# Storing the two parts of a split weight tile with one transfer instead of two, and the scheduler's length for that job halved

## The chip, the cores and the metric

One Trainium2 chip, one of its cores. The metric is the device time of one execution in microseconds (us), as the median of three runs. The engines of the core work side by side, each on its own list of instructions in a fixed order: TensorE (PE) multiplies matrices, VectorE (DVE), ScalarE (ACT) and GpSimd (POOL) do element-wise work, and SyncE (SP) issues nearly all DMA transfers, one after the other. An instruction that has to wait holds up everything behind it on its engine.

## The reference

Linear attention on 8 batches of 8 heads, 576 rows of 64, followed by two MLPs on the 4608 rows of 512 that the attention gives:

```python
q_s = exp(q - max(q, -1)); q_s /= sum(q_s, -1) + 1e-9
k_s = exp(k - max(k, 2));  k_s /= sum(k_s, 2) + 1e-9
kv  = einsum('bhsd,bhse->bhde', k_s, v)
x   = einsum('bhsd,bhde->bhse', q_s, kv)      # to rows of 8 * 64 = 512
h = x @ w_in;  x = (h * clip(h + 3, 0, 6) / 6) @ w_out
h = x @ w2_in; out = (h / (1 + exp(-h))) @ w2_out
```

The weights are float64 on the host (512x2048 and 2048x512 for each MLP), everything is computed at about float32 precision.

## The kernel before

Every operand of a large matrix product is split into a high part, rounded to TensorE's fast float32 form, and a low part, the rest; a product is three matmuls (high by high, high by low, low by high). The 4608 rows are nine blocks of 512 rows. The program has three stages, each written in a fixed order:

- `first_block`: attention of the first rows, conversion of the first MLP's weights, first MLP of block 0.
- `middle`: the first MLP for blocks 1 to 6, one step of 16 after the other (`mm1`, 12 matmuls of 512 columns, then the gate on ACT and DVE, then `mm2`, another 12). Beside it run the attention units of the later blocks (a unit is one block and one pair of heads) and the preparation of the weights for the last stage.
- `second_mlp`: the second MLP of all blocks, and the first one of blocks 7 and 8, by a Strassen-like scheme with seven products for eight. It reads its weights, in quarters and sums of quarters, from a buffer `ws` in HBM.

The weights for that last stage are made in `middle`. `Parts` converts two float64 row groups of the second MLP (`Conv`), `Resident` takes two of the first MLP's, and POOL forms four sums of quarters in place (`sums_in_place`). `Split` then makes the high part (`upper`, ACT), the low part (`lower`, DVE) and stores both (`store`, SP). One `Split` holds two quarters side by side, "halves" of 256 columns; each of them has a place of its own in `ws` (`slot`), and in each place the high part stands left of the low part. So a `store` is four transfers: two halves by two parts.

The order of `middle` comes from a list scheduler, `Plan`. Each job is added with an engine, a length in us, a key (its wanted place in time), the jobs it depends on, and the buffers it takes and gives back. `Plan.once` walks a clock forward and starts on every free engine the ready job of the lowest key whose buffers are free. Lengths in the table thus decide not only when an engine is free but when buffers come back, and so what is started next on every engine. `parted` adds the three jobs of a `Split`; the store's job gives back its `sp` buffers, and for some splits one of the five `t2k` buffers, small scratch tiles that nearly all other jobs share: the copies of a finished block (`finish_copy`, one for each of the four accumulators), the transposed queries (`q_blocks`), and the copies of attention results to be parked in HBM (`x_upper` for blocks from 4 on, tile `xq`).

Three lines of the attention units matter below. `x_mm` (L495) multiplies a unit's queries by its `kv` on PE into one of two PSUM tiles `pa`; `x_upper` (L505) copies that tile out on ACT into an `xq` tile, which frees it; `x_store` (L656) parks the copy. For later units the queries arrive by `q_load` (L479), four DMAs into a tile with the tag `qT`, of which there is one: the next unit's `q_load` has to wait until the `x_mm` that reads the tile is over.

Of the kernel before, what the change touches and what calls it, by code (L numbers as in the profile page):

```python
# [23 lines left out]
def f32(ap):  # L24
    return ap.bitcast(F32)
# [3 lines left out]
def efficient_attention_then_two_mlps(  # L29
# [11 lines left out]
    nc = tc.nc  # L41
# [41 lines left out]
    ws = dram.tile([2, 2, 4 * NF, P, DM], F32, name="ws")  # L83
# [87 lines left out]
    HALF = DM // 2  # L171

    def slot(o, i, part):
        if part == "A21":
            return 7 * NPR + i
        if o:
            return OUTER.index(part) * NPR + i
        if part == "A22":
            return 6 + 7 * i + 2 if i < NPR - 1 else 7 * NPR - 1
        return (0 if i == 0 else 6 + 7 * (i - 1)) + INNER.index(part) + (  # L180
            1 if i and part not in INNER[:2] else 0
        )
# [28 lines left out]
    class Split:  # L211
# [14 lines left out]
            nc.vector.tensor_tensor(out=self.lo, in0=self.src(), in1=f32(self.hi), op=ALU.subtract)  # L226

        def store(self):
            for h, name in enumerate(self.names):
                to = ws[self.ph, self.o, slot(self.o, self.i, name)]  # L230
                for a, t in enumerate((self.hi, self.lo)):
                    nc.sync.dma_start(  # L232
                        to[:, a * HALF : (a + 1) * HALF], f32(t)[:, h * HALF : (h + 1) * HALF]
                    )

    class Parts:

# [475 lines left out]
    class Plan:  # L713
# [7 lines left out]
        def add(self, eng, us, key, fn, deps=(), take=(), give=(), port=False):  # L721
            self.jobs.append(
                (eng, us, key, fn, [d for d in deps if d is not None], list(take), list(give), port)
            )
            return len(self.jobs) - 1
# [265 lines left out]
    def middle():  # L991
# [3 lines left out]
            a=2, h=2, g=1, r=1, z=1, qe=0, qT=1, ke=0, mx=2, m1=1, t2k=5, raw=0, sp=3, x=1, wi=0,  # L995
# [5 lines left out]
        def dma(us, key, fn, kb, deps=(), take=(), give=()):  # L1001
            return add("SP", us, key, (fn, kb * 1024), deps, take, give)
# [69 lines left out]
        def parted(split, key, deps, give=()):  # L1072
            sp = ["sp"] * (1 + split.keep)
            hi = add("ACT", 0.64, key, split.upper, deps, sp)
            lo = add("DVE", 0.72, key, split.lower, [hi], [], [], True)
            st = dma(1.4, key, split.store, 512, [lo], [], sp + list(give))
            return lo if split.keep else st

        for k in range(2 * NPR):
            o, i = divmod(k, NPR)  # L1080
            at = NF + 5.5 * k + 6 + WORK[k]
            p, done = Parts(i, o), []
            for n, c in enumerate(p.conv):
                ld = None
                if k:
                    ld = dma(
                        0.35, at - 2 + n, lambda i=i, n=n, o=o: load_w(1, 2 * i + n, o), 512, [], ["raw"]
                    )
                c0 = add("ACT", 0.67, at + n, c.scale, [ld], ["t2k"])
                c1 = add("DVE", 0.43, at + n, c.shift, [c0])  # L1090
                c2 = add("ACT", 0.67, at + n, c.scale_low, [c0], ["t2k"])
                c2 = add("DVE", 0.72, at + n, c.round, [c1, c2], [], ["t2k"], True)
                c3 = add("DVE", 0.72, at + n, c.sign, [c2], [], ["raw"], True)
                done.append(parted(p.split[n], at + n + 0.2, [c3]))
            for m, fn in enumerate(p.total):
                done = [add("POOL", 0.68, at + 1.3, fn, done, [], [], True)]
            for n in range(2):
                parted(p.split[2 + n], at + 1.4 + n, done, ["t2k"])
# [12 lines left out]
            for n in range(2):  # L1111
                done.append(parted(w.split[n], at + 2.5, done, ["raw"] if n else []))
# [602 lines left out]
```

## Time and profile before

| | us |
|---|---|
| median of three runs | 1578.06 (1576.75 to 1578.68) |
| profiled execution | 1579.01 |
| its span, first to last instruction | 1577.0 |
| PE busy | 1558.9 (99%) |
| DVE, ACT, POOL busy | 1111.1, 761.6, 487.8 |

The profiled execution is an execution of its own, 0.95 us above the median. The span is what the core's instructions cover; 2.0 us lie around it. TensorE ran at its full clock of 2.4 GHz throughout: the granted clock is 1.00. The trace has the start and length of each instruction, so a wait of PE can be read as the gap ahead of a matmul.

### The profile page before, as it was taken

Reading aid. Unit: us, or ns where it says so; the run is one execution under the profiler, and the core shown is the slowest. Engines: PE = TensorE matmul, PEld = TensorE weight load, DVE = VectorE, ACT = ScalarE, POOL = GpSimd, SP = SyncE. Lnnn points to the kernel's source line nnn. Section 1 sums busy time; section 2 is a strip of 40 time slices with the busy share of each in tenths; the row PEclk is TensorE's granted clock in tenths of the full one; section 3 lists DMA queues with packets and bytes.
Section 4 is the critical chain, followed back from the end, with each engine's and each line's share of the span. In section 5 each row is a group of like instructions: output and inputs, shape, how many; then the busy total and the mean of one; then the engine's idle time right before and its main releaser. Section 6 shows DMA issues by size and latency. Waiting matters only on the chain.

```text
span 1577.0 us, 22414 instructions
## 1 busy us (share of the span) xinstructions
PE 1558.9 (99%) x7352; PEld 1268.4 (80%) x7352; DVE 1111.1 (70%) x1792; ACT 761.6 (48%) x1360; POOL 487.8 (31%) x442
## 2 busy tenths in 40 slices
PE   7999999999999999999999999999999999999998
PEld 4777878887878888888888888888888888888887
DVE  7988577776767776554689569846986697677632
ACT  6886245454555554443365236533643464345322
POOL 4334224433424335321232243323223422440000
PEclk9999999999999999999999999999999999999999
DMA  9915977777778875755666786766668875879850
GB/s 267 345 44 185 313 216 227 238 215 215 223 215 246 235 227 166 238 174 193 192 222 218 214 226 224 249 217 192 237 203 218 220 252 192 227 226 370 260 127 27
DMA packets 391203, 342.82 MB, mean 217 GB/s; under 512 B 184880, under 2 KB 297520, under 8 KB 391088
## 3 DMA queue, kind: packets, MB, share of 16 engines
q1 hardware_dynamic: 389040, 340.32, 70.3%
q8 instruction: 58, 0.95, 0.2%
q10 hardware_dynamic: 2048, 1.08, 0.2%
q14 instruction: 57, 0.47, 0.1%
HBM read 247.20 MB, written 94.11 MB: 216 GB/s over the span
## 4 chain that ended last, share of the span: by engine, by line
PE 92%; DMA 2%; issue 1%; DVE 1%; POOL 1%; ACT 1%; SPq 1%; ACTq 0%; POOLq 0%; DVEq 0%
PE pb L1340 24%; PE pb L1499 24%; PE h L541 20%; PE y L613 17%; PE y L615 3%; PE pa L495 2%; PE pa L397 2%; DMA qraw<-in_q_dram 1%; DMA xr<-xq 0%; DMA xq<-xq 0%; POOL wi L164 0%; SPq L232 0%; PE pa L368 0%; PE pa L356 0%; ACT r L554 0%
## 5 line engine op out<-in xcount | busy, mean ns | idle before, releaser
L541 PE MATMUL h<-x,wi 128*128 128x512 f32 x1536 | 382.5, 396 | 1.6 <-POOL wi L164 0.9
L1340 PE MATMUL pb<-xo,ring 128*128 128x512 f32 x1680 | 383.0, 389 | 0.0
L1499 PE MATMUL pb<-gsp,ring 128*128 128x512 f32 x1680 | 382.4, 389 | 0.0
L1340 PEld LDWEIGHTS pb<-xo,ring 128*128 128x128 f32 x1680 | 315.4, 188 | 65.8 <-issue 0.5
L1499 PEld LDWEIGHTS pb<-gsp,ring 128*128 128x128 f32 x1680 | 315.4, 188 | 65.4
L541 PEld LDWEIGHTS h<-x,wi 128*128 128x128 f32 x1536 | 283.5, 188 | 65.9 <-POOL wi L164 2.0
L613 PE MATMUL y<-g,wo 128*128 128x512 f32 x1344 | 323.9, 390 | 0.6 <-ACT g L569 0.6
L613 PEld LDWEIGHTS y<-g,wo 128*128 128x128 f32 x1344 | 251.4, 188 | 53.6 <-ACT g L569 1.1
L1327 DVE TENSOR_TENSOR gsp<-g,gsp 128x512 fp32r<-128x512 f32 x240 | 183.0, 782 | 26.0 <-ACT gsp L1445 25.2
L1445 ACT CAST gsp<-g 128x512 fp32r<-128x512 f32 x240 | 143.6, 621 | 106.2 <-PE pb L1499 88.3
L578 DVE SCALAR_TENSOR_TENSOR h<-r,h 128x512 f32<-128x512 f32 x112 | 77.4, 691 | 80.3 <-ACT r L554 80.1
L554 ACT ACTIVATE r<-h 128x512 f32<-128x512 f32 x112 | 67.0, 598 | 133.4 <-PE h L541 131.7
L1327 POOL TENSOR_TENSOR xst<-xst 128x512 f32<-128x512 f32 x32 | 72.1, 2254 | 167.4 <-DVE xo L1327 85.3
L1327 DVE TENSOR_TENSOR g<-r,pb 128x512 f32<-128x512 f32 x96 | 65.7, 684 | 54.6 <-ACT r L1354 54.1
L1354 ACT ACTIVATE r<-pb 128x512 f32<-128x512 f32 x96 | 57.1, 595 | 97.0 <-DVE pb L1327 72.8
L1327 POOL TENSOR_TENSOR g<-g 128x512 f32<-128x512 f32 x40 | 53.6, 1340 | 148.6 <-DVE g L1327 123.4
L1327 POOL TENSOR_TENSOR s<-U,s 128x512 f32<-128x512 f32 x32 | 42.6, 1331 | 173.1 <-DVE U L1327 173.1
L569 ACT CAST g<-h 128x512 fp32r<-128x512 f32 x112 | 65.6, 586 | 59.8 <-DVE h L578 51.5
L572 DVE TENSOR_TENSOR g<-h,g 128x512 fp32r<-128x512 f32 x97 | 66.7, 688 | 28.8 <-ACT g L569 27.3
L1327 DVE TENSOR_TENSOR U<-pb,s 128x512 f32<-128x512 f32 x80 | 55.0, 688 | 17.0 <-PE pb L1340 14.9
L194 POOL TENSOR_TENSOR fa<-fa 128x256 f32<-128x256 f32 x64 | 49.9, 780 | 43.7 <-DVE sp L226 28.5
L427 POOL TENSOR_TENSOR qe<-qraw,qm 128x512 f32<-128x512 f32 x34 | 37.9, 1114 | 79.4 <-DVE qz L469 46.0
(158 smaller groups left out, 1721.2 us busy)
## 6 DMA issues: line engine op xcount, KB each, us to landing
ring<-ws SPq DMA_DIRECT2D x280, 512.0 KB, 3.9
ws<-sp SPq DMA_DIRECT2D x256, 128.0 KB, 2.6
wi_early<-in_moe_w_in_dram SPq DMA_DIRECT2D x16, 512.0 KB, 8.6
wo_early<-in_moe_w_out_dram SPq DMA_DIRECT2D x16, 512.0 KB, 9.6
wi_raw<-in_moe_w_in_dram SPq DMA_DIRECT2D x16, 512.0 KB, 5.0
ws<-w_sum SPq DMA_DIRECT2D x64, 128.0 KB, 2.2
ws<-fa SPq DMA_DIRECT2D x64, 128.0 KB, 2.3
wo_raw<-in_moe_w_out_dram SPq DMA_DIRECT2D x16, 512.0 KB, 4.4
```

The lines of the kernel that those rows point to most:

```text
L194: lambda to=to, x=x, y=y, op=op: nc.gpsimd.tensor_tensor(out=at[to], in0=at[x], in1=at[y], op=op)
L541: nc.tensor.matmul(h, w[:, a, c, :], x[:, e, c, :], start=(c == 0 and n == 0), stop=(c == NC - 1 and n == 2),)
L554: nc.scalar.activation(self.r, self.h, AF.Relu, bias=3.0)
L569: nc.scalar.copy(self.g[:, 0], self.r)
L572: nc.vector.tensor_tensor(out=self.g[:, 1], in0=self.r, in1=f32(self.g[:, 0]), op=ALU.subtract)
L578: nc.vector.scalar_tensor_tensor(out=self.h, in0=self.r, scalar=6.0, in1=self.h, op0=ALU.min, op1=ALU.mult)
L613: nc.tensor.matmul(y[c], w[:, a, cs], g[:, e, :], start=st, stop=sp)
L1327: (eng or nc.vector).tensor_tensor(out=out, in0=a, in1=b, op=how)
L1340: nc.tensor.matmul(to, ws_[:, a], e[:, c], start=p in ("P1", "P6", "P5") and c == 0 and m == 0, stop=c == 1 and m == 2, skip_group_check=True,
L1354: nc.scalar.activation(r, d[b, n, key], AF.Sigmoid)
L1445: nc.scalar.copy(t[0], source(p, i))
L1499: nc.tensor.matmul(d[b, p][m], w[:, a, m * P : (m + 1) * P], t[e], start=new and i == 0 and k == 0, stop=i == NPR - 1 and k == 2, skip_gro ...
```

## The change

`Split.store` issues two transfers in place of four. Each carries one part of both halves: 128 partitions by 2 places by 256 columns. The destination is a slice of `ws` with a step from the one place to the other. Where the second name's place lies ahead of the first, the halves are read in reverse order. The bytes and the places are the same as before. In the scheduler's table the store's length goes from 1.4 to 0.7 us.

```diff
         def store(self):
-            for h, name in enumerate(self.names):
-                to = ws[self.ph, self.o, slot(self.o, self.i, name)]
-                for a, t in enumerate((self.hi, self.lo)):
-                    nc.sync.dma_start(
-                        to[:, a * HALF : (a + 1) * HALF], f32(t)[:, h * HALF : (h + 1) * HALF]
-                    )
+            s0, s1 = (slot(self.o, self.i, name) for name in self.names)
+            to = ws[self.ph, self.o, min(s0, s1) : max(s0, s1) + 1 : abs(s1 - s0)]
+            to = to.rearrange("s p d -> p s d")
+            for a, t in enumerate((self.hi, self.lo)):
+                halves = f32(t).rearrange("p (h d) -> p h d", h=2)
+                nc.sync.dma_start(
+                    to[:, :, a * HALF : (a + 1) * HALF], halves if s0 < s1 else halves[:, ::-1]
+                )
...
-            st = dma(1.4, key, split.store, 512, [lo], [], sp + list(give))
+            st = dma(0.7, key, split.store, 512, [lo], [], sp + list(give))
```

With the new length the scheduler puts `middle` into another order on all engines. The new code is two lines longer, so line numbers from `store` on are two higher in the rows of the changed kernel (L495 becomes L497, L541 L543, L613 L615).

PE, the end of the first MLP's block 5 and the start of block 6, before. `y_5800` to `y_5803` are the accumulators of block 5, `y_6705` and on those of block 6; `pa<-qt` is an `x_mm`, and the number behind `kv` tells the units apart (97, 96 and 93 are three that follow each other):

```order
L613 MATMUL y_5803<-g,wo 128x512
L541 MATMUL h<-x,wi 128x512 x12
L613 MATMUL y_6705<-g,wo 128x512
...
L495 MATMUL pa<-qt,kv_97 128x512
L541 MATMUL h<-x,wi 128x512 x12
...
L495 MATMUL pa<-qt,kv_96 128x512
L541 MATMUL h<-x,wi 128x512 x12
...
L495 MATMUL pa<-qt,kv_93 128x512
L541 MATMUL h<-x,wi 128x512 x12
```

The same place of the changed kernel; `y_5695` is block 5's last accumulator there, `y_6679` block 6's first:

```order
L615 MATMUL y_5695<-g,wo 128x512
L543 MATMUL h<-x,wi 128x512 x24
L497 MATMUL pa<-qt,kv_97 128x512
L543 MATMUL h<-x,wi 128x512 x12
L497 MATMUL pa<-qt,kv_96 128x512
L497 MATMUL pa<-qt,kv_93 128x512
L615 MATMUL y_6679<-g,wo 128x512
```

Before, the three `x_mm` stood 66 and 40 rows apart inside block 6, with many `mm1` and `mm2` between them. Now they stand between the last `mm2` of block 5 and the first of block 6, one group of 12 matmuls between the first and the second and none between the second and the third.

SP at that place, in the changed kernel (`qt<-zd` is a `q_load`, the first one here for the second of these `x_mm`, the second one for the third; `yd<-o` stores a copy of `finish_copy`, `xq<-xq` is an `x_store`):

```order
L481 DMA qt<-zd 32x16x32 x4
L637 DMA yd<-o 128x512
L234 DMA ws<-sp 128x2x256
L234 DMA ws<-w_sum 128x2x256
L1205 DMA xo<-yd 128x2x512 x2
L234 DMA ws<-sp 128x2x256 x2
L481 DMA qt<-zd 32x16x32 x4
L637 DMA yd<-o 128x512
```

Before, the four `yd<-o` of block 5 stood in one group, and the `q_load`s beside them belonged to units whose `x_mm` came later. Now a `q_load` stands ahead of two of the `yd<-o`. The ACT copy (L507) that frees the `pa` tile of kv_97 waits for the landing of the last `yd<-o` shown, whose `t2k` buffer it writes into.

PE at the end of block 3, before (`k_turn` is L356, `k_spread` L368; between them DVE takes a maximum):

```order
L356 MATMUL pa<-ident,peaks 128x128
L495 MATMUL pa<-qt,kv_97 128x4x80
L495 MATMUL pa<-qt,kv_96 128x4x48
L541 MATMUL h<-x,wi 128x512 x3
L368 MATMUL pa<-ident,small 128x128
L541 MATMUL h<-x,wi 128x512 x9
```

and now:

```order
L543 MATMUL h<-x,wi 128x512 x12
L358 MATMUL pa<-ident,peaks 128x128
L370 MATMUL pa<-ident,small 128x128
L497 MATMUL pa<-qt,kv_97 128x4x80
L497 MATMUL pa<-qt,kv_96 128x4x48
L615 MATMUL y_4735<-g,wo 128x512
```

The `k_spread` follows its `k_turn` directly, and the `x_mm` follows the `k_spread`.

## Rows read from the trace of the kernel before

**Rows 1.** The page: the span, and busy time of each engine.

```profile
span 1577.0 us, 22414 instructions
PE 1558.9 (99%) x7352; PEld 1268.4 (80%) x7352; DVE 1111.1 (70%) x1792; ACT 761.6 (48%) x1360; POOL 487.8 (31%) x442
```

**Rows 2.** Busy time in stretches: us, each engine's busy time, PEclk, DMA share, GB/s.

```profile
130.00:600.00 470.00, 465.95 (x2415) 375.85 (x2412) 335.33 (x608) 233.33 (x427) 179.99 (x208) 1.00 0.78 233
600.00:722.00 122.00, 122.00 (x562) 98.75 (x561) 69.52 (x99) 55.24 (x94) 42.05 (x40) 1.00 0.57 178
750.00:1400.00 650.00, 650.00 (x2869) 538.41 (x2868) 484.46 (x705) 295.53 (x522) 208.97 (x135) 1.00 0.72 219
```

**Rows 3.** Who waited for whom, PE, 130 to 722 us: total, times, longest.

```profile
PE pa L356 <- DVE peaks L351: 2.6, 2, 2.1
PE y L613 <- ACT g L569: 0.6, 1, 0.6
PE pa L397 <- ACT ke L387: 0.4, 1, 0.4
PE pa L368 <- DVE small L362: 0.4, 1, 0.4
```

**Rows 4.** The page's DMA issues: count, KB each, median us to landing.

```profile
ws<-sp SPq DMA_DIRECT2D x256, 128.0 KB, 2.6
ws<-w_sum SPq DMA_DIRECT2D x64, 128.0 KB, 2.2
ws<-fa SPq DMA_DIRECT2D x64, 128.0 KB, 2.3
```

**Rows 5.** Timeline of SP, 150 to 200 us: start, length, instructions.

```profile
171.19 5.29 SPq L206 DMA_DIRECT2D ws<-wo  x8
176.59 2.08 SPq L232 DMA_DIRECT2D ws<-sp  x4
```

**Rows 6.** Landing of the stores of line L232 (the three groups of rows 4).

```profile
DMA to landing us min/median/max: 1.7/2.4/6.5
```

**Rows 7.** Landing of the stores of line L206 (256 KB each).

```profile
DMA to landing us min/median/max: 2.4/2.6/4.2
```

**Rows 8.** Timeline of PE, 595 to 722 us: start, length, instructions.

```profile
638.52 2.88 PE L613 MATMUL y<-g,wo 128*128 128x512 f32 x12
641.24 2.88 PE L541 MATMUL h<-x,wi 128*128 128x512 f32 x12
...
652.13 1.02 PE L495 MATMUL pa<-qt,kv 128*128 128x512 f32 x2
652.59 3.32 PE L541 MATMUL h<-x,wi 128*128 128x512 f32 x12
655.74 2.88 PE L613 MATMUL y<-g,wo 128*128 128x512 f32 x12
...
697.45 1.02 PE L495 MATMUL pa<-qt,kv 128*128 128x512 f32 x2
```

**Rows 9.** Timeline of SP, 600 to 722 us: the load behind the last x_mm.

```profile
698.50 2.83 SPq L479 DMA_DIRECT2D qt<-zd  x4
```

**Rows 10.** Line L479: duration ns min/median/max, first and last start us; landing.

```profile
L479 SPq DMA_DIRECT2D qt<-zd x108: 557/634/1432, 188.4 to 700.7; - x108
...
DMA to landing us min/median/max: 2.2/2.7/6.0
```

**Rows 11.** Landing of the stores of line L635 (yd<-o).

```profile
DMA to landing us min/median/max: 2.1/3.1/7.7
```

**Rows 12.** Timeline of ACT, 610 to 660 us: the idle time ahead in brackets.

```profile
653.24 0.59 ACT L505 COPY xq<-pa 128x512 f32<-128x512 f32 x1 [1.42 <-PE pa L495]
```

**Rows 13.** Timeline of PE, 425 to 470 us.

```profile
435.94 0.33 PE L356 MATMUL pa<-ident,peaks 128*128 128x128 f32 x1 [0.53 <-DVE peaks L351]
...
464.19 0.30 PE L356 MATMUL pa<-ident,peaks 128*128 128x128 f32 x1 [2.07 <-DVE peaks L351]
```

**Rows 14.** Timeline of PE, 130 to 137 us.

```profile
134.76 0.27 PE L356 MATMUL pa<-ident,peaks 128*128 128x128 f32 x1
135.42 0.32 PE L368 MATMUL pa<-ident,small 128*128 128x128 f32 x1 [0.38 <-DVE small L362]
```

**Rows 15.** Timeline of DVE, 130 to 137 us.

```profile
135.78 0.82 DVE L377 TENSOR_TENSOR ke<-kbuf,pa 128x640 f32<-128x640 f32 x1 [0.31 <-PE pa L368]
```

**Rows 16.** The page's groups: busy us, mean ns of one, idle before.

```profile
L578 DVE SCALAR_TENSOR_TENSOR h<-r,h 128x512 f32<-128x512 f32 x112 | 77.4, 691 | 80.3 <-ACT r L554 80.1
```

## The prediction

> **What bounds the kernel.** I read the page's busy times first: PE is busy 1558.9 us of 1577.0 [rows 1], so the other engines and the DMA queues count only where they make PE wait. The busy times by stretch tell where that can be: from 750 to 1400 us PE has no idle time at all, and from 600 to 722 none either [rows 2]. The order of the last stage and the order of the first do not change. What is left is `middle`, roughly 130 to 722 us, and there the view of who waited for whom shows all that PE loses to waits: 2.6 + 0.6 + 0.4 + 0.4 = 4.0 us, and none of it directly for a DMA [rows 3]. So nothing that the change makes cheaper can give back more than 4.0 us. What it can cost has no such limit, because PE works through its list in order and a wait that the new order creates stays in the time: the last stage has no idle time to absorb it.
>
> **The stores themselves.** The three groups of stores are 384 transfers of 128 KB [rows 4]; they become 192 of 256 KB. SP needs 2.08 us for the four of one split, and 5.29 / 8 = 0.66 us for one 256 KB store of another kind [rows 5]. Two of the new form are not in the trace; taking that row they cost 1.3 us, and the saving is 0.75 us for each of 96 splits, some 72 us of SP's time over 590. From the other side, if a new store cost as much as two old ones, nothing is saved. Either way PE gains 0 from it directly: none of its waits is for SP or for a store, and the 4.0 us above are the most that can come back. Landing hardly moves: 2.4 us at the median for a 128 KB store, 2.6 for a 256 KB store [rows 6, 7].
>
> The page "DMA: Bandwidth & Descriptors" of the Trainium skill, section "Rules for kernel authors", says to merge many small transfers into one large one, and its section "Anatomy of one DMA" gives each transfer a fixed cost of about 2.0 us. An estimate from that page of the Trainium skill would be one fixed cost less for each pair of stores. The trace bears out that the landing has a large fixed part, since twice the bytes land only 0.2 us later [rows 6, 7], but here the two old stores of a pair overlap, issued about 0.5 us apart [rows 5]: as their landings overlap, that fixed part is not saved per pair, and what the Trainium skill's page promises would show as a gain only where somebody waits for the landing. That is the first rival below.
>
> **The order, end of block 5.** Here the change costs. The three `x_mm` of kv_97, kv_96 and kv_93 now stand close together, and the queries of each arrive through the single `qT` tile. The price of one turn of that tile is in the trace. An `x_mm` started at 697.45 [rows 8]; SP began the next unit's four loads at 698.50 [rows 9], 1.05 us later, when PE had read the tile. The four took 2.83 us to issue, the last of them starting at 700.7; a load lands 2.2 us after its start at the least and 2.7 at the median [rows 10]. So the next `x_mm` cannot start before 700.7 + 2.7 - 697.45 = 5.95 us after the one before it (5.45 with the fastest landing). On PE an `x_mm` fills 0.89 us: from 652.13 to 655.74 it and 12 matmuls take 3.61, and 12 matmuls alone take 641.24 - 638.52 = 2.72 [rows 8].
>
> - Second `x_mm` (kv_96): between it and the first stand 12 matmuls. PE waits 5.95 - 0.89 - 2.72 = 2.34 us (1.84 with the fastest landing).
> - Third (kv_93): nothing stands between. By the tile alone PE waits 5.95 - 0.89 = 5.06 us (4.56). But it also needs a PSUM tile, and of the two one still holds the result of kv_97. The ACT copy that frees it waits for a `t2k` buffer, and that for the landing of the `yd<-o` store which SP issues behind the third's loads. The chain, from the start of the second `x_mm`: 1.05 until SP may load, 2.83 for the four issues, 3.1 for a `yd<-o` to land (2.1 at the least), 0.59 for the copy [rows 9, 11, 12], and two hand-overs, from the landing to the copy and from the copy to PE. I estimate one at 0.09: the copy at 653.24 began that much after the `x_mm` of 652.13 had run its 1.02 [rows 8, 12]. That makes 7.75 us; less 0.89, PE waits 6.9 us.
>
> What stands behind the third `x_mm` on PE is the whole of block 6; its first `mm2`s have their inputs ready, and are held up all the same. I take 2.34 + 6.9 = 9.2 us. At the least it is 1.84 + 4.56 = 6.4. At the most, with landings at the long end seen (6.0 for the load, 7.7 for the store), it is some 3.3 and 4.6 more, 17 us.
>
> **The order, end of block 3.** Before, PE waited here twice for the `k_turn`, 0.53 and 2.07 us, because DVE's maximum was late [rows 13]. The order of DVE around it changes too, and I let both go: -2.6. In their place `k_spread` follows its `k_turn` directly. That pattern is in the trace: the starts stand 0.66 us apart with nothing between, a little of which is the matmul's own [rows 14], so 0.6. The `x_mm` behind it needs the PSUM tile of that `k_spread`, which is free when DVE's subtraction has read it: it began 0.36 us after the `k_spread` and took 0.82 [rows 14, 15], 1.2 us; a gate step of DVE that comes ahead of it can add up to its 0.69 [rows 16]. I take 1.6, and so +2.2. Together -0.4; bounds are -2.6, if DVE turns out early and nothing new arises, and +2.2, if the old waits stay as well.
>
> **Sum.** 9.2 - 0.4 = 8.8 us. The remaining 1.4 us of old waits [rows 3] I leave as they are; elsewhere in `middle` the new order moves single `x_mm` and `k` steps by a few matmuls, with neighbours between them that cover a turn, and I count these at 0, with 1 us either way. The profiled execution took 1579.01, so it would be 1587.8; it lay 0.95 above the median of the runs, so the median becomes 1586.9, rounded to 1587.
>
> **Rivals.**
>
> - Faster. SP is freed of up to 72 us, the transfers that feed DVE and ACT start earlier, and the 4.0 us of old waits go. This is where the Trainium skill's page "DMA: Bandwidth & Descriptors", section "Rules for kernel authors", would lead. For it: SP is the busiest issuer and stands in order. Against it: the three `x_mm` above. It decides where a `qT` turn fits into what PE has between two `x_mm`, that is below 0.89 us for the last pair; 5.45 us is the fastest that the rows give. Time: 1578.1 - 4.0 = 1574. Chance 3%.
> - No change that can be told (0.2%, 3.2 us, is about what a measurement of this kernel can tell). The block's end costs its least, 6.4, and the 4.0 of old waits go entirely: +2.4, 1580.5. It needs the PSUM tile of kv_97 to be freed early, so that only the `qT` turn counts, and landings at their fastest. Chance 7%.
> - Clearly slower still: the burst of stores, loads and copies at the block's end finds the queue full, landings come at their long end, and the scheduler, which believes a store to be over 0.7 us sooner than before, hands out buffers too early in other places. Then 9.2 goes towards 17 and the end of block 3 towards +2.2: up to 1597; as a case of its own I price it at +15, 1593. For it: SP's landings reach 6.0 and 7.7 us [rows 10, 11]. Against it: the DMA engines are 57% busy in that stretch [rows 2]. Chance 20%.
>
> **Chances and range.** The forecast, 1583 to 1590, has 70%. The low end of the range, 1581, leaves out the faster rival and most of the one without change; the high end, 1596, leaves out the tail of the dear one. Slower by over 0.2% is the forecast and the dear rival, 0.90; within 0.2% 0.07; faster 0.03.
>
> **What would show it.** In the profile after, PE's timeline at the end of block 5 (somewhat beyond 635 us) should show two gaps, each ahead of an L497 of full width: about 2 us, and 5 to 8 us; and the second should be ended by ACT's copy L507 or by `qt<-zd`. PE's waits in `middle` should add up to about 13 us in place of 4.0, the last stage still without idle time, and the whole stage shifted. The waits of L356 at the end of block 3 should be replaced by a short one ahead of L370 and one ahead of an L497. I am wrong if these gaps are below 3 us in all, if the third `x_mm` finds its queries early, or if the time lost is spread over other places.

## The result and the profile after

The changed kernel takes 1593.3 us at the median of three runs (1592.7 to 1594.6), the kernel before 1578.4. The ratio is 1.0097 (95% interval 1.0077 to 1.0117): slower by about 15 us, where 9 were forecast. A fourth run, of 5571 us, is left out of both. In the changed kernel's lines the numbers from L232 on are larger by 2.

The page of the kernel after: the span, PE's busy time, and the largest group of stores in its new form.

```profile
span 1591.0 us, 22121 instructions
...
PE 1563.3 (98%) x7352; PEld 1271.0 (80%) x7352; DVE 1112.8 (70%) x1792; ACT 760.3 (48%) x1360; POOL 490.0 (31%) x442
...
ws<-sp SPq DMA_DIRECT2D x128, 256.0 KB, 3.2
```

The span grew by 14.0 us against [rows 1], and PE's busy time by 4.4 us for the same 7352 matmuls: some of them ran slower. (1.3 us of that lie in the first 43 us, where PE is busy 35.09 us in place of 33.80; `middle` still began at the same time, within 0.1 us.) The 384 stores are now 192, and the median landing of the largest group rose from 2.6 [rows 4] to 3.2 us.

The same stretches as [rows 2], their ends moved to the same places in the work:

```profile
130.00:600.00 470.00, 467.09 (x2424) 377.24 (x2420) 339.67 (x612) 232.89 (x428) 188.80 (x216) 1.00 0.78 235
600.00:737.00 137.00, 124.87 (x561) 99.76 (x560) 66.99 (x94) 55.34 (x95) 34.83 (x32) 0.95 0.52 161
765.00:1415.00 650.00, 650.00 (x2869) 538.25 (x2868) 485.31 (x705) 296.40 (x524) 208.98 (x135) 1.00 0.71 219
```

Where PE had no idle time at the end of `middle`, it now lacks 137 - 124.87 = 12.1 us, at a clock of 0.95; the last stage is as full as before. Who PE waited for, 120 to 745 us (total, times, longest), to be set beside [rows 3]:

```profile
PE pa L497 <- ACT xq L507: 9.7, 1, 9.7
PE pa L497 <- DMA qt<-zd: 1.9, 1, 1.9
PE pa L497 <- DVE ke L379: 1.4, 1, 1.4
PE pa L370 <- DVE small L364: 0.8, 2, 0.4
PE pa L370 <- ACT xq L507: 0.6, 1, 0.6
PE pa L399 <- ACT ke L389: 0.4, 1, 0.4
PE pa L399 <- ACT xq L507: 0.3, 1, 0.3
```

Together 15.1 us in place of 4.0. PE's timeline at the end of block 5 shows the first two:

```profile
646.49 1.10 PE L497 MATMUL pa<-qt,kv 128*128 128x512 f32 x2 [1.88 <-DMA qt<-zd]
657.28 2.07 PE L497 MATMUL pa<-qt,kv 128*128 128x512 f32 x2 [9.69 <-ACT xq L507]
658.36 10.69 PE L615 MATMUL y<-g,wo 128*128 128x512 f32 x36
668.89 2.88 PE L543 MATMUL h<-x,wi 128*128 128x512 f32 x12
```

The two gaps stand where the prediction put them and end as it said. Beside them is a loss that it did not have. An `x_mm` and the 36 matmuls behind it fill 0.89 + 3 x 2.72 = 9.05 us by [rows 8]; here, from the third `x_mm` to the next L543, they took 668.89 - 657.28 = 11.61. The clock says why (busy time in stretches, PEclk the third number from the end):

```profile
646.00:648.00 2.00, 1.10 (x2) 0.30 (x2) 1.25 (x2) 0.00 (x0) 1.28 (x2) 1.00 1.03 356
648.00:650.00 2.00, 0.00 (x0) 0.00 (x0) 0.69 (x1) 0.62 (x1) 1.84 (x3) 0.69 0.89 211
...
660.00:662.00 2.00, 2.00 (x6) 1.61 (x5) 0.00 (x0) 0.00 (x0) 0.00 (x0) 0.50 0.88 281
662.00:664.00 2.00, 2.00 (x9) 1.60 (x9) 0.00 (x0) 0.37 (x1) 0.00 (x0) 0.89 0.63 104
```

In the gap the granted clock fell to 0.50, its lower level of 1.2 GHz, and up to 662 us it was still there, though PE worked again from 657.3. That cost 11.61 - 9.05 = 2.6 us. Waits and clock add up: 15.1 - 4.0 + 2.6 = 13.7 of the 14.0 us of span.

Why the third `x_mm` was so late is read from SP and ACT. SP's timeline:

```profile
646.23 1.12 SPq L1205 DMA_DIRECT2D xo<-yd  x2
647.45 0.98 SPq L234 DMA_DIRECT2D ws<-sp  x2
648.52 4.92 SPq L481 DMA_DIRECT2D qt<-zd  x4
653.55 0.96 SPq L637 DMA_DIRECT2D yd<-o  x1
```

and ACT's:

```profile
654.12 1.24 ACT L223 CAST sp<-fa 128x512 fp32r<-128x512 f32 x2 [5.20 <-DMA ws<-sp]
656.64 0.59 ACT L507 COPY xq<-pa 128x512 f32<-128x512 f32 x1 [1.27 <-DMA yd<-o]
```

The `qT` loads began 648.52 - 646.49 = 2.03 us after the second `x_mm`, not 1.05, because SP was still issuing two stores, which stood behind two loads of 512 KB for the last stage (`xo<-yd`). The four issues took 4.92 us, not 2.83. Behind them the chain went as forecast: `yd<-o` was issued at 653.55 and the copy began 3.1 us later. The DMA's view of 644 to 658 us has the share of the 16 engines' time that the queue's packets took, and the median us to landing of the loads:

```profile
q1 hardware_dynamic: 6741, 3.92, 97.7%
...
xo<-yd SPq DMA_DIRECT2D x2, 512.0 KB, 6.1
...
qt<-zd SPq DMA_DIRECT2D x5, 64.0 KB, 5.1
```

The loads of the queries, behind those of 512 KB, landed 5.1 us after their issue at the median, where [rows 10] have 2.7.

### The profile page after: what moved, and what is told of

It reads as the page before. It is cut to its first block, busy times and chain, and to the rows that moved or that the text cites. A ratio compares the mean times of both kernels' runs of the same rounds, so it can differ in the third digit from the quotient of the medians.

```text
span 1591.0 us, 22121 instructions
## 1 busy us (share of the span) xinstructions
PE 1563.3 (98%) x7352; PEld 1271.0 (80%) x7352; DVE 1112.8 (70%) x1792; ACT 760.3 (48%) x1360; POOL 490.0 (31%) x442
## 3 DMA queue, kind: packets, MB, share of 16 engines
q10 hardware_dynamic: 2048, 1.08, 0.2%
## 4 chain that ended last, share of the span: by engine, by line
PE 95%; issue 1%; ACT 1%; DMA 1%; POOL 1%; SPq 1%; DVE 0%; ACTq 0%; POOLq 0%
PE pb L1501 24%; PE pb L1342 24%; PE h L543 21%; PE y L615 19%; PE y L617 3%; PE pa L497 2%; PE pa L399 1%; POOL wi L164 0%; SPq L481 0%; DMA wi_early<-in_moe_w_in_dram 0%; PE pa L370 0%; PE pa L463 0%; DMA qraw<-in_q_dram 0%; PE pa L358 0%; DMA yd<-o 0%
## 5 line engine op out<-in xcount | busy, mean ns | idle before, releaser
L543 PE MATMUL h<-x,wi 128*128 128x512 f32 x1536 | 381.2, 396 | 1.7 <-POOL wi L164 0.9
L543 PEld LDWEIGHTS h<-x,wi 128*128 128x128 f32 x1536 | 283.6, 188 | 64.9 <-POOL wi L164 1.9
L615 PE MATMUL y<-g,wo 128*128 128x512 f32 x1344 | 326.4, 393 | 0.0
L615 PEld LDWEIGHTS y<-g,wo 128*128 128x128 f32 x1344 | 252.7, 189 | 54.8 <-issue 1.0
L1356 ACT ACTIVATE r<-s 128x512 f32<-128x512 f32 x32 | 20.2, 633 | 87.3 <-POOL s L1329 70.3
```

What stands on the lines that cost most here:

```text
L543: nc.tensor.matmul(h, w[:, a, c, :], x[:, e, c, :], start=(c == 0 and n == 0), stop=(c == NC - 1 and n == 2),)
L615: nc.tensor.matmul(y[c], w[:, a, cs], g[:, e, :], start=st, stop=sp)
L1356: nc.scalar.activation(r, d[b, n, key], AF.Sigmoid)
```

## Experiments

Ratios are to the kernel before, with their 95% intervals.

**The table alone** (`e1_table_only`): the old four stores, the length 0.7.

```
-            st = dma(1.4, key, split.store, 512, [lo], [], sp + list(give))
+            st = dma(0.7, key, split.store, 512, [lo], [], sp + list(give))
```

> The new length in the table alone: the four 128 KB stores of a split stay, the order of the work is that of the changed kernel. Theory (the order makes the time: PE waits at the end of block 5 for the single qT tile and for the ACT copy that frees its PSUM tile): about 1594 us, at most 3 us above it, since SP also has twice the stores to issue there; a wait of 8 us or more ahead of the third x_mm. Rival (the two-place stores themselves are dear, by longer landings or by the queue): the time goes back towards 1578 to 1583 us, and that wait shrinks below 5 us.

Measured: 1602.0 us, ratio 1.0142 (1.0126 to 1.0158). Its longest waits of PE:

```profile
PE pa L495 <- ACT xq L505: 10.0, 1, 10.0
PE y L613 <- ACT g L569: 4.7, 4, 2.7
```

The order makes the loss, and the rival falls. But it is slower than the theory allowed (at most 3 us above 1594), by 5 us: with 384 stores four waits for gates appear, one of them 2.7 us. In this order the new stores are worth 7 us by the ratios, 9 by the medians.

**The stores alone** (`e2_stores_only`): the changed kernel with the length 1.4, so two transfers per split in the order of before.

```
-            st = dma(0.7, key, split.store, 512, [lo], [], sp + list(give))
+            st = dma(1.4, key, split.store, 512, [lo], [], sp + list(give))
```

> The merged stores alone: the length in the table stays 1.4, so the order of the work is that of the kernel before. Theory (the order makes the time): 1575 to 1579 us, the kernel before or up to 3 us better, no gap above 4 us at the end of block 5, and PE's waits in the middle stage 4 us or less. Rival (the two-place stores are dear): 1585 to 1594 us, with PE waits that end on copies or matmuls waiting for the landing of a ws store.

Measured: 1574.8 us, ratio 0.9977 (0.9967 to 0.9987): at the low edge of what the theory expected, faster than both kernels, and the version to keep. PE's waits from 120 to 760 us are two:

```profile
PE pa L399 <- ACT ke L389: 0.4, 1, 0.4
PE pa L370 <- DVE small L364: 0.4, 1, 0.4
```

The two waits for DVE's peaks [rows 13] are gone with the order unchanged. What held them in the kernel before is read by following the second one back, from the end of the chain to its start (DVE, ACT, DVE, POOL, each a row of its timeline):

```profile
462.36 0.69 DVE L663 TENSOR_TENSOR x<-xr,x 128x512 fp32r<-128x512 f32 x1 [3.04 <-ACT x L659]
```

```profile
461.23 0.59 ACT L505 COPY xq<-pa 128x512 f32<-128x512 f32 x1 [3.50 <-DMA zd<-qz]
```

```profile
454.57 0.71 DVE L469 STREAM_TRANSPOSE qz<-qe 128x512 f32<-128x512 f32 x1 [3.34 <-POOL w_sum L194]
```

```profile
448.73 2.55 POOL L269 TENSOR_TENSOR w_sum<-wo 128x512 f32<-128x512 f32 x2 [14.38 <-DMA ws<-w_sum]
```

DVE came to the peaks only after L663, which waited for ACT; ACT's cast stood behind a copy that waited for the store `zd<-qz` to land; what it stores is DVE's transpose, which waited for sums of POOL; and POOL had waited 14.38 us for a `ws<-w_sum` store, one of those that the change merges. With merged stores POOL waits 12.45 us there, the transpose 0.2, and the same ACT copy:

```profile
455.81 0.59 ACT L507 COPY xq<-pa 128x512 f32<-128x512 f32 x1 [0.50 <-DMA zd<-qz]
```

By SP's and DVE's rows there, SP had issued the last of these stores 446.75 - 441.26 = 5.5 us after DVE had made what it stores; with merged stores it is 441.83 - 438.85 = 3.0. That the shorter issue is the cause is a reading of two traces; the next run puts it to the test.

**As many issues as before** (`e14_padded`): the version above, with a store of one row behind each merged store.

```
...
+                nc.sync.dma_start(pad[padded[0]], f32(t)[0:1, 0:HALF])
```

> The merged stores with the length 1.4 (the order of the kernel before), and behind each of the 192 merged stores a store of one row of 1 KB to a place that nobody reads, so that SP issues as many transfers as the kernel before while the bytes and the form of the merged stores stay. Theory (the 4 us that the merged stores gave came from SP's time: SP reached other transfers earlier): the gain goes, 1577.5 to 1580 us, and PE's waits for L353's peaks at the end of block 3 are back. Rival (the gain lies in the DMA queues: fewer or longer descriptors): 1574 to 1576 us.

Measured: 1577.0 us, 0.9986 (0.9977 to 0.9994), between both expectations, and its interval touches that of the stores alone. ACT waits for `zd<-qz` 2.4 us, between 3.5 before and 0.5:

```profile
ACT xq L511 <- DMA zd<-qz: 2.4, 1, 2.4
```

but PE's wait for the peaks is 0.3 us, not 2.6. The small stores cost more than SP's time: they read the same tiles, and POOL's wait, 13.77 us here, now ends with the landing of one of them. About half of the gain is left all the same, so SP's issue time is at most a part of it; how much stays open.

**The third `x_mm` later** (`e3_third_later`): one unit moved by hand in the finished list of work.

```
...
+        move([("x_mm", 34), ("q_load", 35), ("x_upper", 34), ("x_store", 34)], ("mm1", ((0, 6, 5), 0)))
...
```

> The changed kernel, with the third x_mm (kv_93), the load of the queries behind it and its finish moved by hand from the end of block 5 to before the sixth group of matmuls of block 6; nothing else is moved. Theory of the prediction (the third x_mm's own turn of qT and PSUM is the whole loss): the 9.7 us wait goes, the clock stays at full speed, 1581 to 1583 us. Rival (several works are equally late there: SP's stores, the t2k buffers that the splits hold, the finish copies that wait for landings, and the x_mm is only the first to show it): PE waits a few matmuls further on for a tile of block 6 instead, the sum of its waits stays above 10 us, 1591 to 1596 us.

Measured: 1594.7 us, 1.0103 (1.0089 to 1.0116): nothing gained, as the rival says. The wait has only moved, to block 6's first matmuls:

```profile
PE y L615 <- DVE o L634: 10.1, 2, 9.7
```

The finish copy of block 5 that frees their PSUM tile is as late as the `x_mm` was. On DVE it stands behind two instructions of L226, which wait for ACT's casts of L223, and those for the landing of a `ws` store:

```profile
655.85 3.22 DVE L226 TENSOR_TENSOR fa<-fa,sp 128x512 fp32r<-128x512 f32 x2 [4.91 <-ACT sp L223]
659.05 0.69 DVE L634 TENSOR_SCALAR o<-y 128x512 f32<-128x512 f32 x1
```

**Six `t2k` buffers** (`e5_six`).

```
...
-            return tmp.tile([P, BLK], F32, tag=tag, bufs=1 if tag == "r" else 5, name=name)
+            return tmp.tile([P, BLK], F32, tag=tag, bufs=1 if tag == "r" else 6, name=name)
```

> The changed kernel with six t2k buffers in place of five, the order unchanged. Theory A (the ACT copy that ends the 9.7 us wait stands for a t2k buffer, that is for the landing of a yd store): the copy no longer waits for yd, the third x_mm then waits for the queries by qT alone, some 5 us in place of 9.7 and a shorter time at half clock: 1586 to 1589 us. Theory B (the loads of the third's queries are as late as the copy, because SP reached them late and took 4.92 us to issue them): the wait is still 8 to 9.5 us, ended by the landing of qt<-zd, 1592 to 1594 us.

Measured: 1590.4 us, 1.0077 (1.0064 to 1.0091), between what the two theories expected. The long wait is 8.5 us and now ends with the loads, as theory B says:

```profile
PE pa L497 <- DMA qt<-zd: 10.3, 2, 8.5
```

So the copy and the queries were late within 1.2 us of each other.

**The last stage's loads later** (`e9_sums_later`).

```
...
+        move([("load", "B22"), ("load", "B11")], ("load", "B21"))
...
```

> The changed kernel, with two loads of 512 KB (xo<-yd, the operands B22 and B11 of the last stage) moved by hand from SP's list just ahead of the third x_mm's queries to about 20 us later; the order of all else is unchanged. Theory (full DMA engines and SP's own list make the third x_mm later than its tile alone): SP reaches the loads of the queries some 1 us earlier, the four issues take near 2.8 us in place of 4.92, the wait ahead of the third x_mm is 6 to 7.5 us, the time at half clock is shorter: 1588.5 to 1591.5 us. Rival (the copy that frees the PSUM tile stands behind splits whose store lands late for another reason): the wait stays 9 to 10 us, 1593 to 1595 us.

Measured: 1590.6 us, 1.0074 (1.0059 to 1.0089), as the theory says. In this trace all of `middle` stands 2.5 us later than in the changed kernel's, so only differences of times are to be compared. On SP and ACT:

```profile
651.02 2.61 SPq L481 DMA_DIRECT2D qt<-zd  x4
```

```profile
651.86 1.21 ACT L223 CAST sp<-fa 128x512 fp32r<-128x512 f32 x2 [0.67 <-DMA ws<-sp]
```

and on PE:

```profile
649.05 1.94 PE L497 MATMUL pa<-qt,kv 128*128 128x512 f32 x2 [1.94 <-DMA qt<-zd]
656.97 2.08 PE L497 MATMUL pa<-qt,kv 128*128 128x512 f32 x2 [5.99 <-ACT xq L507]
```

Without that 1 MB the four issues take 2.61 us, though the queue's packets still take 90.4% of the engines' time in the same 14 us (646.5 to 660.5 there); ACT's casts wait 0.67 in place of 5.20, and the third `x_mm` starts 7.92 us after the second (10.79 in the changed kernel, 7.75 forecast). One part missed: SP's loads still begin 1.97 us behind the second `x_mm`, which itself took 1.94 us at a clock of 0.79 in 648 to 650 us.

**Four suspects at once** (`e12_four_remedies`): the two moves above, six buffers, and

```
...
+        move([("finish_copy", (5, 0)), ("finish_copy", (5, 2)), ("finish_store", (5, 0)), ("finish_store", (5, 2))], ("x_mm", 32))
...
```

> The changed kernel with all suspects at the end of block 5 eased at once: six t2k buffers, the two loads of 512 KB later, the third x_mm later, and the two finish copies with their stores ahead of the second x_mm. Theory (several chains are equally late there, each gives little alone, together most): a single wait of 3 to 5 us is left ahead of block 6's matmuls, no time at half clock, 1582 to 1587 us. Rival (the cause is none of these, say the shorter length's effects elsewhere): 1590 us or more.

Measured: 1585.1 us, 1.0037 (1.0023 to 1.0052). What is left at the end of block 5:

```profile
PE y L615 <- ACT g L571: 2.6, 1, 2.6
PE pa L497 <- DMA qt<-zd: 2.1, 1, 2.1
```

The sum of the waits is 4.7 us there, as expected, but in two pieces, and the clock still fell, there (0.69 from 656 to 660 us) and at the end of block 3 (0.67 from 448 to 452). About 9 of the 15 us are recovered, where single remedies gave 0 to 3.5.

**PE kept busy in the gap** (`e13_filled`): 32 matmuls ahead of the third `x_mm`, whose results are overwritten.

```
...
+            nc.tensor.matmul(
+                y[c], wo[0, 0][:, 0, c * P : (c + 1) * P], gt[0, 6, 0][:, 0, :], start=True, stop=True
+            )
...
+            if name_of(fn) == ("x_mm", 34):
+                fill(32)
```

> The changed kernel, with 32 extra matmuls of 128x512 just ahead of the third x_mm; they write two PSUM tiles of block 6 that its first matmul overwrites afterwards, and so take some 7.3 us of PE's idle 9.7 us (32 at 2.72 us for 12). Theory (about 3 us of the loss is TensorE's lower clock after the idle time): the granted clock stays at full speed over the end of block 5, the 36 matmuls of L615 behind it take 8.2 to 8.5 us in place of 10.69, the third x_mm starts no later than before: 1590 to 1592 us. Rival (the clock falls for another reason, or the fill delays the third x_mm): 1593.5 us or more.

Measured: 1591.6 us, 1.0075 (1.006 to 1.0091), below the changed kernel by 1.7 us in the medians and 3.5 in the ratios. PE and the clock (two stretches):

```profile
648.62 9.15 PE L623 MATMUL y<-g,wo 128*128 128x512 f32 x32
658.37 1.12 PE L497 MATMUL pa<-qt,kv 128*128 128x512 f32 x2 [0.61 <-ACT xq L507]
658.93 8.92 PE L615 MATMUL y<-g,wo 128*128 128x512 f32 x36
667.69 2.88 PE L543 MATMUL h<-x,wi 128*128 128x512 f32 x12
```

```profile
648.00:650.00 2.00, 2.00 (x4) 0.88 (x4) 0.69 (x1) 0.54 (x1) 1.76 (x4) 0.50 1.01 263
...
652.00:653.00 1.00, 1.00 (x6) 0.83 (x5) 0.00 (x0) 0.00 (x0) 0.04 (x1) 1.00 1.02 365
```

From the third `x_mm` to the next L543 it takes 667.69 - 658.37 = 9.32 us in place of 11.61, so 2.3 us less, and the third `x_mm` starts 10.63 us after the second, nearly as late as ever (10.79): the saving is the clock. The time and the start came as the theory says; two parts missed. The 36 matmuls show 8.92 us, not 8.2 to 8.5, of which 0.4 is the overlap with the `x_mm` that they follow. And the clock did not stay up: it was 0.50 from 648 to 650 us, behind the gap of 2.2 us, but back at 1.00 from 652 us on, while the fill ran.

**Other lengths** (`len11`, `len09`): the merged stores with 1.1, as here, and with 0.9 in the table.

```
-            st = dma(0.7, key, split.store, 512, [lo], [], sp + list(give))
+            st = dma(1.1, key, split.store, 512, [lo], [], sp + list(give))
```

> The merged stores with 1.1 in the table, between 1.4 and 0.7. Theory (the time depends on which works an order happens to put together at a block's end, not on how true the length is): 1574 to 1580 us, waits of less than 2 us at a time. Rival (the shorter the length, the earlier buffers are handed out, the slower): between 1574.8 and 1593.9, about 1583 us.

> The merged stores with 0.9 in the table, twice the 0.45 us that SP took to issue one of the new stores in the trace, so the truest length for SP. Theory (what an order puts together decides): 1580 to 1588 us, with waits of 3 to 5 us ahead of L615 at the end of block 5, and so slower than with 1.1 although the length is truer. Rival (a true length gives the best order): at or below the 1574.8 us of the length 1.4.

Measured: 1578.1 us, 0.9995 (0.9986 to 1.0005), and 1591.9 us, 1.0081 (1.0066 to 1.0096). With 1.1 the kernel stands as before; 0.9 costs 13 us, more than the 1588 us at most that were expected. I had called 0.9 the truest length by one store of 0.45 us. The median of the largest group in the changed kernel is 0.54 (in ns, the second of three):

```profile
L234 SPq DMA_DIRECT2D ws<-sp x128: 359/539/1787, 150.3 to 696.8; - x128
```

Two of them take 1.08 us, so for SP the truest of the four is 1.1, and it is better than 0.9 and 0.7, but not the best. In the four, the shorter the length, the slower the kernel, though by steps and not in proportion (1.1 was put at 1583 by that rival). A length above 1.4 was not tried. The losses of 0.9 are again at the end of block 5, here at the finish copies:

```profile
PE y L615 <- ACT o L632: 9.2, 2, 6.4
```

## Why the prediction was right, and where its size was off

- **The time: inside the range of 1581 to 1596, above the forecast's own 1583 to 1590.** 1593 is what the dear rival (20%) was priced at. Its mechanism came in part: issues and landings of the queries' loads were late, while the `yd<-o` that ends the chain landed as usual. That the sum stayed in the range is partly luck, as two terms put at nothing, the clock and the gain of the merged stores, have opposite signs.
- **Sign, place and form: right.** The two gaps, their order and what ends them came as forecast. Second `x_mm`: 2.34 forecast, 1.88 measured.
- **End of block 3: right.** Forecast -2.6 + 2.2 = -0.4. The waits of L356 are gone; in their place the waits show 0.4 ahead of L370 and 1.4 ahead of the `x_mm`, -0.8. The second one in the starts (PE's timeline) is 449.03 - 447.32 = 1.71, less the matmul's own 0.32:

```profile
447.32 0.32 PE L370 MATMUL pa<-ident,small 128*128 128x128 f32 x1 [0.38 <-DVE small L364]
449.03 1.13 PE L497 MATMUL pa<-qt,kv 128*128 128x320 f32 x4 [1.38 <-DVE ke L379]
```

- **Third `x_mm`: the term that was mis-sized, 6.9 forecast, 9.69 measured.** The chain was the right one. Two of its links were not: "1.05 until SP may load" was 2.03, and "2.83 for the four issues" was 4.92. 0.98 + 2.09 = 3.07 us, and 7.75 + 3.07 = 10.82 is the 10.79 measured from one `x_mm` to the next. Both links were taken from the row at 698.50 [rows 9], where nothing else was queued; here two loads of 512 KB and four stores were issued in the 4 us ahead. That burst was in the new order, but I weighed it with the mean of 57% over 122 us [rows 2] and so called it unlikely. In the 14 us that count the queue was at 97.7%. That share alone does not make the issues long (90.4% in the run without the two loads): moving the two loads away brought the four issues to 2.61 and the chain to 7.92 us.
- **The clock: a term left out, 2.6 us.** I reckoned only with the wait. The Trainium skill's page "TensorE: Matmul & The Clock Gate", section "HAM oscillation — how this bites in real kernels", describes a wait for a DMA after which the next burst of matmuls runs at the lower clock. This trace agrees, with a wait that ended with ACT's copy: 0.50 from inside the gap until 662 us, and 2.3 us of PE's time there came back when PE was kept busy.
- **"Held up all the same" was too simple.** I took the third `x_mm` as the only late thing. Moved away, it uncovers a finish copy that is late by as much. The loss belongs to a knot of chains (queries, `t2k` buffers, splits waiting for their stores, finish copies). That one backlog of SP and the DMA queue stands behind them all is how I read it; no run shows it, and with all four remedies some 6 us of the loss are left.
- **"PE gains 0 from it directly": wrong, and hidden.** The stores alone give about 4 us in the old order and 7 to 9 in the new one, so the order's own price is some 19 to 23 us, not 8.8. The bound, that at most 4.0 us can come back in the old order, held as far as can be told. I had read that no wait of PE was for a store [rows 3], but the peaks that PE waited for hung on one four steps further back. The rule of the Trainium skill's page "DMA: Bandwidth & Descriptors", section "Rules for kernel authors", to merge small transfers, was right for this kernel where the order stayed. The first rival's 1574 is what the stores alone reach (1574.8).
- **"Landing hardly moves": wrong.** I set 2.4 us for the old stores beside 2.6 for stores of another line [rows 6, 7]. All stores of the changed line landed after 3.2 us at the median (3.4 in the stores alone), 0.8 later than before. No term of the sum used it.

## What to carry to other kernels

A number in a scheduler's table is a request for another order, and the truest is not always the best: here 1.4, 1.1, 0.9 and 0.7 gave 1575, 1578, 1592 and 1593 us with the same instructions, where SP took 1.08, so change the transfer and the table apart, and time both. Price a wait with what is queued at that very place on the issuing engine and in the DMA engines, not with a quiet row or a mean over a stage, and add the matmuls that run slower behind it. And before an edit is called free, follow each wait that is left back beyond the engine it names.

## What the runs showed of the hardware

- A 256 KB store to two places cost SP 0.54 us to issue at the median of `ws<-sp` in the changed kernel, an old one of 128 KB 0.44 in the kernel before: twice the bytes, a quarter more time. I had taken 0.66 and 0.52.
- The issue of four 64 KB loads took 2.61 to 2.83 us, also where the DMA share was high (2.61 from 641.88 us of the changed kernel, 0.97 in 642 to 644), and 4.92 with two loads of 512 KB and two stores just ahead of them (4.91 in the filled kernel).
- In the gap of 9.7 us the granted clock fell to its lower level, and it stayed there while PE worked from 657.3 to 662 us; with matmuls run in that gap it was back at full speed before the gap's end. A gap of about 2 us can be enough, but need not be: behind 1.94 us (the loads later) and 2.22 us (the filled gap) the second `x_mm` took 1.94 and 1.86 us, behind 2.12 us (four remedies) 1.10, as at full clock.
